# Another order of the same 578 pieces: layer norm, local dilated attention and a gelu MLP on one core

## The chip, the cores and the metric

The kernel runs on one core of one Trainium2 chip. The metric is the device time of one execution in microseconds, lower is better. The median of six runs of the kernel before is 212.39 us (212.2 to 212.59).

## What is computed

One layer-normed input feeds an attention branch and an MLP branch, and both are added to the input:

```python
xn = _layernorm(x)                       # x: 2048 x 640, bf16
# A: q, k, v = xn @ wqkv; 32 heads of 20; each position looks at itself and at
#    the 7 positions 2, 4, ... 14 before it (W = 8, dilation 2), softmax over these 8
logits = einsum("bhsd,bhswd->bhsw", q, kg) * scale
attn   = softmax(where(mask, logits, -1e9))
o      = einsum("bhsw,bhswd->bhsd", attn, vg);   A = o @ wo
# B: 640 -> 1536 -> 640
B      = gelu(xn @ w1 + b1) @ w2 + b2
return x + A + B
```

## The kernel before

The 2048 positions are cut into four chunks of 512, numbered 0 to 3 (n), and each chunk into four blocks of 128 (bl). Features lie on the partitions, positions along the free axis. Everything runs in small **pieces**, Python functions that each issue a few instructions. The list ORDER (from line 84) names every piece once, and the last lines of the kernel simply call the pieces in that order. Four engines (PE, DVE, ACT, SP) take their instructions in exactly the order of the list; each engine runs its own instructions strictly one after another, and semaphores make an instruction wait for what it needs from other engines. Only POOL is outside this: its instructions are placed by the framework. So ORDER fixes what each engine does next, and with it which instruction stands behind a waiting one.

Names of pieces that the text below uses (first digit: the chunk):

- `st`, `rs`, `rc`, `xn`: statistics (DVE), square root (ACT), reciprocal (DVE), normalised block (DVE for chunk 0, ACT for the others). `tp`, `tc` turn a block: on PE and by copies for chunk 0, by a DMA transpose on SP's queue for chunks 1 to 3 (line 477), into `xnT`.
- Projections: `pj{n}{q,k,v = 0,1,2}{to}` is five matmuls of 128x512 (line 509), and `pc...` is the ACT copy out of PSUM (line 568). In chunk 0 they are cut finer: `ga`, `gb*`, `gd`, `ge`, then `hj{q,k,v}{pair}{g}` of five or ten matmuls of 128x256 (line 553), with ACT copies `hc...` and `gc...`. `pad` fills the 14 columns that reach back into the chunk before.
- Attention on DVE: `qk{n}{w}{i}` multiplies q by the shifted k (line 583), eight per chunk; `lg{n}0` to `lg{n}3` sum over each head on PE (line 608); `m`, `mx`, `ex` (ACT), `ss`, `ri`, `at` are the softmax; `xd` (SP's queue) and `xs` (ACT's queue), two DMAs each at line 665, spread the weights `ax` over the 20 partitions of a head; `av` (eight, line 681), `ad` (three, line 690) and `ot` (line 696) form the attention output `oT`.
- MLP: `f1{n}{ft}` is five matmuls of 128x512 (line 703) and `ge{n}{ft}` the gelu on ACT (line 714).
- Output: `o{n}{bl}0` to `o{n}{bl}4` accumulate block bl in two PSUM banks `lo` and `hi` (lines 734 and 736); pieces 0 to 3 take three gelu tiles each, piece 4 takes `oT`, so piece 4 of the first block of a chunk waits for `ot`. `oc` (ACT, lines 741 and 742) copies out, `od` (POOL, line 747) adds the block to the output in DRAM. `xp` and `xb` put x and b2 into the output before that. The last block ends the kernel with `oclo`, `ohi` and `ochi`.

Buffers: four PSUM banks are shared by all `pj`, `f1` and `hj` outputs, so PE may run at most four such pieces ahead of ACT's copies. `lo`, `hi` and the logits have one place each. The products `prod` of `qk` and `av` share four buffers; `ax`, `oT` and the softmax tiles have one.

Weights come in at the start on SP's queue in the fixed order x block 0, wq, wk, x blocks 2 and 3, wv, the rest of x, w1 in two halves (from line 342). ACT needs a table load whenever it goes between square root, exp and gelu.

The lines that make the list into a program:

```python
        pieces = make_plan(fns).by
        assert sorted(ORDER) == sorted(pieces)
        for name in ORDER:
            pieces[name]["fn"]()
```

Of the kernel before, what the change touches and what calls it, by code (L numbers as in the profile page):

```python
# [82 lines left out]

ORDER = """
pad01 pad02 st00a st00 sm rs00 me nm rc00 sq xn00a xn00b tp00a tp00b tc00a rs01 tb ga tc00b rc01 xn01 gb2 b1 tp01
gb3 tc01a tc01b gb4 gd gc0 ge st03a hj101 gc4 st03 st02a rs03 hj102 st02 hc101 hj100 rs02 hc102 rc02 rc03 gc1 hj200
xn03 xn02 hc100 st11a tp03 tp02 st13a tc03 hj201 st11 tc02 st10a hj202 hc200 st12a hj012 st10 hj010 st13 hc012 hc202
st12 hj111 hc010 hc201 hj011 rs1 hc111 rc1 st21a hj110 hc011 st22a st22 hj112 hc110 st20a hj212 st33a hc112 f102
xn10 qk031 hc212 f100 xn13 tc10 qk001 ge02 f109 qk020 hj210 pad11 tc13 ge09 hj211 qk010 xn11 f108 hc211 qk000 ge00
f101 tc11 qk011 f105 ge01 ge08 qk021 f104 xn12 f1011 tc12 ge04 qk030 f1010 ge011 st23a st21 lg00 ge010 st20 ld lg01  # L90
ge05 st23 lg02 lg03 st31a rs2 pj114 mk m0 pj102 pc114 st32a st30a pj110 pc102 mx0 hc210 pj111 pc110 st32 ex0 pj101
rc2 st31 st30 pj100 st33 pj112 ss0 pc100 pc101 pj104 xn21 ri0 pj103 tc21 pc104 at0 pc111 pj113 pc103 pc112 pj123
pc113 xn23 qk120 f113 pc123 tc23 xn22 f103 qk111 pj121 ge03 qk121 f118 xd0 qk130 ge13 f107 ge18 f112 qk100 ge07
pad21 f106 ge12 qk110 xs0 f115 ge06 qk131 xw0 f110 rs3 qk101 o020 tc22 xn20 o021 ge15 lg10 lg11 av011 lg12 pc121
tc20 lg13 ge10 rc3 pj120 av000 o022 pc120 av031 xn32 o023 pj122 tc32 av021 f111 pc122 m1 xn30 pj124 ge11 av030 tc30
pad12 pj214 av020 pj204 pc214 pj203 pc204 av001 pj211 pc203 av010 pc124 pj202 xn33 mx1 pc211 pj210 tc33 xn31 ad01
pj221 pc210 pc202 pj223 tc31 pj201 ad00 pj220 pc201 pc223 pj213 xp0 pj200 pc213 ad02 pc221 pj212 pc220 pc200 pj224
pc212 ex1 xb0 ot0 pj310 f1110 qk231 pc310 o024 qk220 pj300 oc02 ss1 pad31 od02 o000 o001 qk200 o002 o003 ri1 o004
at1 pj313 qk201 xd1 oc00 o010 pc313 qk211 pc300 pj301 xs1 qk210 o011 o012 qk221 o013 xw1 pj303 qk230 o014 xp1 xb1
lg20 oc01 lg21 av130 pc303 lg22 pc224 lg23 av100 o030 f138 av110 o031 od00 ge38 av111 pj312 o032 pc301 m2 ge110 f117  # L100
pc312 av131 f116 av120 pj304 pj302 mx2 o033 pc302 av121 ge16 f121 ge17 ad11 f1111 xp2 f1210 ge21 xb2 ge111 o034
ge210 av101 pad22 pc304 f119 ad10 pj311 pj222 pc311 xb3 oc03 pj314 ad12 ge19 od01 f114 od03 f125 ge14 pc222 ot1
pj324 pad32 pc314 ex2 o100 qk331 pj322 qk321 o101 ge25 o102 ss2 o103 pj323 ri2 o104 qk330 pc323 pc322 pj320 at2 oc10
pj321 pc320 qk311 xd2 xs2 o110 pc324 qk301 o111 pc321 o112 qk310 f120 qk300 f126 xw2 f130 ge26 qk320 f127 xl lg30
ge27 lg31 av201 lg32 lg33 o113 m3 o114 av211 f1311 oc11 av200 od11 o120 o121 od10 av221 o122 av230 o123 o124 av220
f1211 oc12 mx3 od12 o130 av210 o131 ge20 ge30 f124 ex3 ad20 f123 o132 ge311 o133 av231 o134 ge24 ss3 f128 ge211 oc13
f129 ad21 ge23 f122 ge29 ge28 f131 ge22 ri3 o210 at3 f135 ad22 o211 xd3 f134 f1310 ot2 o212 ge310 ge31 o213 xs3 o214
xw3 f137 oc21 ge34 od21 o220 av311 o221 o222 av300 o223 av310 o224 f136 av321 oc22 od22 o230 av301 o231 od13 o232
av320 o233 av331 o234 av330 f132 oc23 od23 o200 ad31 o201 ge32 ge36 o202 ge37 f139 ad30 f133 ge39 ge35 o203 ge33
o204 ad32 o310 oc20 o311 o300 ot3 o301 o302 o303 o304 o312 oc30 o313 od30 o320 od20 o321 o322 o323 o314 o324 oc31  # L110
od31 o330 oc32 o331 od32 o332 o333 o334 ohi oclo ochi
""".split()


# [696 lines left out]
```

## Time and profile before

| | before |
| --- | --- |
| median of six runs (lowest, highest) | 212.39 us (212.2, 212.59) |
| the profiled execution | 212.2 us |
| its span, first to last instruction | 210.2 us |
| PE matmuls busy | 205.2 us, 98% of the span |
| DVE busy | 173.4 us, 82% |
| ACT busy | 111.6 us, 53% |
| POOL busy | 19.8 us, 9% |
| DMA traffic | 23.93 MB, mean 114 GB/s |

The span is what the trace covers; 2.0 us of the profiled execution's time lie around it. Busy times of engines overlap. A PE row's duration is that of one matmul from start to end, and matmuls are pipelined, so the distance from one start to the next, not the duration, is what a matmul costs in a row of them. In the rows of the timeline, the first column is the start in us, the second the time from the first start to the last end, and a bracket at the end says how long the engine stood idle before and what ended it.

### The profile page before, as it was taken

The page shows a single profiled execution, that of the slowest core. Times are in us where ns is not written, and L with a number is a line of the kernel's source. Part 1 is how long each engine was busy: PE and PEld are TensorE (multiplying, and loading weights), DVE is VectorE, ACT ScalarE, POOL GpSimd, SP SyncE. Part 2 cuts the span into 40 slices and gives each one's busy share as a digit, 9 for nine tenths or more (in the row PEclk, how much of TensorE's full clock was granted, in tenths as well). Part 3 has the DMA queues.
Part 4 walks back from the last instruction along what each step waited for, and adds up shares of the span by engine and source line. Part 5 has one row for each costly group of instructions (what it writes and reads, how often), then busy time and mean ns, then how long its engine had stood idle before and what let it go on. Part 6 is the DMA issues. An engine that isn't in the chain of part 4 may idle for free.

```text
span 210.2 us, 3645 instructions
## 1 busy us (share of the span) xinstructions
PE 205.2 (98%) x1511; PEld 118.5 (56%) x1535; DVE 173.4 (82%) x178; ACT 111.6 (53%) x193; POOL 19.8 (9%) x37
## 2 busy tenths in 40 slices
PE   8999999999999999999999999999999999999994
PEld 2999646554465555555654555565554455555552
DVE  3587999969979999996999999969999929997001
ACT  5477977899785849230717486321396221441120
POOL 2000000000000002110400600101101011101130
PEclk9999999999999999999999999999999999999999
DMA  6999427915862074569296790731212572212224
GB/s 216 366 362 372 91 36 203 379 44 92 139 65 54 9 189 46 84 95 232 64 153 219 97 152 3 122 110 11 27 27 34 100 125 18 28 27 31 31 25 72
DMA packets 24072, 23.93 MB, mean 114 GB/s; under 512 B 9080, under 2 KB 21880, under 8 KB 24056
## 3 DMA queue, kind: packets, MB, share of 16 engines
q1 hardware_dynamic: 17008, 14.68, 26.4%
q0 software_dynamic: 4144, 4.92, 17.7%
q10 hardware_dynamic: 2904, 4.10, 7.1%
q8 instruction: 12, 0.20, 0.4%
q14 instruction: 4, 0.03, 0.1%
HBM read 10.00 MB, written 7.54 MB: 83 GB/s over the span
## 4 chain that ended last, share of the span: by engine, by line
PE 96%; DMA 1%; issue 1%; ACT 1%; DVE 0%
PE lo L734 27%; PE hps L703 25%; PE pps L509 23%; PE hi L736 8%; PE gps L553 6%; PE L L608 4%; PE gps L522 1%; DMA x_sb<-in_A_x_dram 1%; PE tp L465 1%; ACT xn L417 0%; DVE xn L450 0%; ACT std L430 0%; DVE osb L764 0%; DVE rstd L434 0%; ACT L376 0%
## 5 line engine op out<-in xcount | busy, mean ns | idle before, releaser
L703 PE MATMUL hps<-xnT,w_sb 128*128 128x512 bf16 x235 | 55.1, 379 | 0.3
L681 DVE TENSOR_TENSOR pv<-vT,ax 128x2560 bf16<-128x2560 bf16 x32 | 45.9, 1485 | 9.2 <-DMA ax<-attn 8.0
L734 PE MATMUL lo<-w_sb,hT 128*128 128x512 bf16 x184 | 52.9, 379 | 0.1
L583 DVE TENSOR_TENSOR prod<-qT,kT 128x2560 bf16<-128x2560 bf16 x32 | 45.5, 1485 | 1.9 <-ACT kT L568 1.5
L714 ACT ACTIVATE hT<-hps,b1T 128x512 bf16<-128x512 f32 x48 | 31.6, 688 | 19.9 <-PE hps L703 18.5
L736 PE MATMUL hi<-w_sb,hT 128*128 128x128 bf16 x192 | 40.3, 219 | 0.5 <-issue 0.2
L703 PEld LDWEIGHTS <-w_sb 128*128 128x128 bf16 x240 | 22.8, 98 | 26.1 <-DMA w_sb<-in_B_w_dram 0.3
L690 DVE TENSOR_TENSOR pv<-pv 128x5120 bf16<-128x5120 bf16 x12 | 33.7, 2822 | 0.2
L741 ACT CAST osb<-lo 128x512 bf16<-128x512 f32 x15 | 8.8, 586 | 44.7 <-issue 26.7
L734 PEld LDWEIGHTS <-hT 128*128 128x128 bf16 x192 | 18.7, 98 | 22.5 <-issue 0.4
L734 PE MATMUL lo<-wo,oT 128*128 128x512 bf16 x74 | 21.9, 379 | 0.0
L747 POOL DMA_DIRECT2D out_dram<-osb x15 | 13.6, 904 | 86.4 <-ACT osb L742 80.2
L736 PEld LDWEIGHTS <-hT 128*128 128x128 bf16 x192 | 18.4, 98 | 2.7
L509 PE MATMUL pps<-xnT,wk_sb 128*128 128x512 bf16 x73 | 18.2, 379 | 0.1
L509 PE MATMUL pps<-xnT,wv_sb 128*128 128x512 bf16 x72 | 18.0, 379 | 0.1
L509 PE MATMUL pps<-xnT,wq_sb 128*128 128x512 bf16 x75 | 18.0, 379 | 0.1
L736 PE MATMUL hi<-wo,oT 128*128 128x128 bf16 x80 | 16.9, 219 | 0.3
L409 DVE BATCH_NORM_STATS2 stats<-x_sb 128x6 f32<-128x320 bf16 x30 | 13.0, 468 | 4.4 <-DMA x_sb<-in_A_x_dram 4.4
L490 POOL DMA_DIRECT2D out_dram<-b2bc x4 | 5.3, 1466 | 98.1 <-DMA out_dram<-x_sb 98.1
L568 ACT CAST qT<-pps 128x512 bf16<-128x512 f32 x15 | 8.7, 590 | 8.8 <-PE pps L509 8.8
L734 PEld LDWEIGHTS <-oT 128*128 128x128 bf16 x80 | 7.8, 98 | 9.4
L509 PEld LDWEIGHTS <-wk_sb 128*128 128x128 bf16 x75 | 8.6, 118 | 7.3 <-issue 0.2
(75 smaller groups left out, 198.5 us busy)
## 6 DMA issues: line engine op xcount, KB each, us to landing
w_sb<-in_B_w_dram SPq DMA_DIRECT2D x4, 960.0 KB, 11.1
out_dram<-osb POOLq DMA_DIRECT2D x15, 160.0 KB, 3.4
ax<-attn SPq DMA_DIRECT2D x8, 256.0 KB, 4.7
ax<-attn ACTq DMA_DIRECT2D x8, 256.0 KB, 4.3
out_dram<-b2bc POOLq DMA_DIRECT2D x3, 640.0 KB, 6.7
x_sb<-in_A_x_dram SPq DMA_DIRECT2D x1, 1280.0 KB, 13.6
out_dram<-x_sb ACTq DMA_DIRECT2D x1, 1120.0 KB, 4.6
wq_sb<-in_A_wqkv_dram SPq DMA_DIRECT2D x1, 800.0 KB, 4.8
```

The lines of the kernel that those rows point to most:

```text
L409: nc.vector.bn_stats(stats[:, i, :], x_sb[:, b, i * (D // 2) : (i + 1) * (D // 2)])
L509: nc.tensor.matmul(ps[:], lhsT=wqkv_p[which][:, ti, to, :], rhs=xnT[:, ti, :], start=(ti == 0), stop=(ti == KT - 1),)
L553: nc.tensor.matmul(ps[:, to - a, :], lhsT=wqkv_p[which][:, ti, to, :], rhs=tiles["xnT", 0][:, ti, pair * 2 * P : (pair + 1) * 2 * P], star ...
L583: nc.vector.tensor_tensor(out=prod[:, i, :, :], in0=qkv_tile(n, 0)[:], in1=qkv_tile(n, 1)[:, :, off : off + CH], op=ALU.mult,)
L681: nc.vector.tensor_tensor(out=pv[:, i, :, :].rearrange("p t (j c) -> p t j c", j=BPC), in0=qkv_tile(n, 2)[:, :, off : off + CH].rearrange( ...
L690: nc.vector.tensor_tensor(out=ta[:], in0=ta[:], in1=tb[:], op=ALU.add)
L703: nc.tensor.matmul(ps[:], lhsT=w1_sb[:, ti, ft * P : (ft + 1) * P], rhs=tiles["xnT", n][:, ti, :], start=(ti == 0), stop=(ti == KT - 1),)
L714: nc.scalar.activation(hT[:], tiles["hps", n, ft][:], ACT.Gelu_apprx_tanh, bias=b1T[:, ft : ft + 1], scale=1.0)
L734: nc.tensor.matmul(lo[:], lhsT=lhs, rhs=rhs[:, 0:CH], start=first, stop=last)
L736: nc.tensor.matmul(hi[:, 0 : D - CH], lhsT=lhs, rhs=rhs[:, CH:D], start=first, stop=last)
L741: nc.scalar.copy(osb[:, 0:CH], tiles["lo", n, bl][:])
L747: nc.gpsimd.dma_start(rows, tiles["osb", n, bl][:], accum_op=ALU.add)
```

## The change

Only the text of ORDER differs. The same names stand in it, each once, so every instruction is issued once as before, on the same engine, with the same operands. What changes is which comes after which on PE, DVE, ACT and SP, and through the rotating buffers which piece waits for which. The first 33 names are the same (up to `hj101`), and so are the last ten. Pieces that the text below speaks of, cut out of both lists (the numbers of the chunks are the first digits):

```diff
-gb3 tc01a tc01b gb4 gd gc0 ge st03a hj101 gc4 st03 st02a rs03 hj102 st02 hc101 hj100 rs02 hc102 rc02 rc03 gc1 hj200
+gb3 tc01a tc01b gb4 gd gc0 ge st03a hj101 gc1 st03 st02a rs03 hj100 st02 hc101 gc4 rc03 xn03 hj200 rs02 hc100 rc02
...
-pc113 xn23 qk120 f113 pc123 tc23 xn22 f103 qk111 pj121 ge03 qk121 f118 xd0 qk130 ge13 f107 ge18 f112 qk100 ge07
-pad21 f106 ge12 qk110 xs0 f115 ge06 qk131 xw0 f110 rs3 qk101 o020 tc22 xn20 o021 ge15 lg10 lg11 av011 lg12 pc121
+pc100 f112 pc113 xs0 qk121 f106 xd0 f118 qk120 ge06 f103 qk101 f107 ge03 qk130 pad21 f110 ge07 xw0 xn21 o020 qk100
+ge18 pj121 xn22 qk111 pj123 tc22 qk131 o021 pc123 ge12 f113 qk110 pc121 rs3 f115 tc21 lg10 ge10 rc3 lg11 av020 lg12
...
-at1 pj313 qk201 xd1 oc00 o010 pc313 qk211 pc300 pj301 xs1 qk210 o011 o012 qk221 o013 xw1 pj303 qk230 o014 xp1 xb1
+od00 pj310 qk210 xd1 o010 pc310 pj300 qk201 o011 qk230 pj313 o012 pc313 qk231 xs1 o013 o014 qk220 xw1 pj301 xp1 lg20
...
-pj324 pad32 pc314 ex2 o100 qk331 pj322 qk321 o101 ge25 o102 ss2 o103 pj323 ri2 o104 qk330 pc323 pc322 pj320 at2 oc10
-pj321 pc320 qk311 xd2 xs2 o110 pc324 qk301 o111 pc321 o112 qk310 f120 qk300 f126 xw2 f130 ge26 qk320 f127 xl lg30
+pc312 f126 ge210 ri2 f127 at2 ge26 o101 pc321 qk331 xd2 o102 pj324 ot1 f121 qk310 o103 o104 qk330 pj320 oc10 qk301
+ge27 od10 o110 qk321 pj222 o111 qk320 pc222 pc320 f130 xs2 qk311 f120 pc324 xw2 o112 qk300 f138 lg30 ge38 lg31 av231
...
-f129 ad21 ge23 f122 ge29 ge28 f131 ge22 ri3 o210 at3 f135 ad22 o211 xd3 f134 f1310 ot2 o212 ge310 ge31 o213 xs3 o214
-xw3 f137 oc21 ge34 od21 o220 av311 o221 o222 av300 o223 av310 o224 f136 av321 oc22 od22 o230 av301 o231 od13 o232
+at3 o134 ad20 xd3 f124 oc13 xs3 od13 f123 pad32 od11 f135 ge23 ad22 ge24 f134 ge29 o210 xw3 ge34 o211 ot2 o212 o213
+xl av321 o214 av320 f137 oc21 od21 o220 av301 o221 av331 o222 o223 av311 o224 av310 f136 oc22 od22 o230 av300 o231
```

Engine by engine this comes to the following. PE runs the q piece `hj102` and a v piece `hj212` later in chunk 0, so the first v piece `hj200` is two pieces (ten and ten matmuls) behind `ge` instead of three; from there the projections, `f1` and `o` pieces stand in other places, with the four `lg` groups after the same amount of PE work as before. DVE takes the softmax of chunk 1 (`m1`, `mx1`) after the attention output of chunk 0 instead of between its products, the sums, reciprocals and weights of chunk 2 (`ss2`, `ri2`, `at2`) before `ot1` instead of after it, and those of chunk 3 (`ss3`, `ri3`, `at3`) directly after the products of chunk 2, ahead of its `ad20` and `ad22`. SP issues `xd0` after one transpose of chunk 2 instead of two, and `xp0` between the transposes of chunk 3 instead of after them. ACT has `xs0`, `xs1`, `xs2`, `xs3` at new places, and `xs0` now stands directly before a gelu with a table load. ACT loads a table 12 times after the first in either order. POOL's sequence of output DMAs is the same.

More of the change, by code (lines that the diff above doesn't have):

```diff
@@ L85 @@
 pad01 pad02 st00a st00 sm rs00 me nm rc00 sq xn00a xn00b tp00a tp00b tc00a rs01 tb ga tc00b rc01 xn01 gb2 b1 tp01
-gb3 tc01a tc01b gb4 gd gc0 ge st03a hj101 gc4 st03 st02a rs03 hj102 st02 hc101 hj100 rs02 hc102 rc02 rc03 gc1 hj200
-xn03 xn02 hc100 st11a tp03 tp02 st13a tc03 hj201 st11 tc02 st10a hj202 hc200 st12a hj012 st10 hj010 st13 hc012 hc202
-st12 hj111 hc010 hc201 hj011 rs1 hc111 rc1 st21a hj110 hc011 st22a st22 hj112 hc110 st20a hj212 st33a hc112 f102
-xn10 qk031 hc212 f100 xn13 tc10 qk001 ge02 f109 qk020 hj210 pad11 tc13 ge09 hj211 qk010 xn11 f108 hc211 qk000 ge00
@@ L90 @@
-f101 tc11 qk011 f105 ge01 ge08 qk021 f104 xn12 f1011 tc12 ge04 qk030 f1010 ge011 st23a st21 lg00 ge010 st20 ld lg01
-ge05 st23 lg02 lg03 st31a rs2 pj114 mk m0 pj102 pc114 st32a st30a pj110 pc102 mx0 hc210 pj111 pc110 st32 ex0 pj101
-rc2 st31 st30 pj100 st33 pj112 ss0 pc100 pc101 pj104 xn21 ri0 pj103 tc21 pc104 at0 pc111 pj113 pc103 pc112 pj123
-pc113 xn23 qk120 f113 pc123 tc23 xn22 f103 qk111 pj121 ge03 qk121 f118 xd0 qk130 ge13 f107 ge18 f112 qk100 ge07
-pad21 f106 ge12 qk110 xs0 f115 ge06 qk131 xw0 f110 rs3 qk101 o020 tc22 xn20 o021 ge15 lg10 lg11 av011 lg12 pc121
@@ L95 @@
[L95 to L98, printed above, removed]
-at1 pj313 qk201 xd1 oc00 o010 pc313 qk211 pc300 pj301 xs1 qk210 o011 o012 qk221 o013 xw1 pj303 qk230 o014 xp1 xb1
@@ L100 @@
-lg20 oc01 lg21 av130 pc303 lg22 pc224 lg23 av100 o030 f138 av110 o031 od00 ge38 av111 pj312 o032 pc301 m2 ge110 f117
-pc312 av131 f116 av120 pj304 pj302 mx2 o033 pc302 av121 ge16 f121 ge17 ad11 f1111 xp2 f1210 ge21 xb2 ge111 o034
-ge210 av101 pad22 pc304 f119 ad10 pj311 pj222 pc311 xb3 oc03 pj314 ad12 ge19 od01 f114 od03 f125 ge14 pc222 ot1
-pj324 pad32 pc314 ex2 o100 qk331 pj322 qk321 o101 ge25 o102 ss2 o103 pj323 ri2 o104 qk330 pc323 pc322 pj320 at2 oc10
-pj321 pc320 qk311 xd2 xs2 o110 pc324 qk301 o111 pc321 o112 qk310 f120 qk300 f126 xw2 f130 ge26 qk320 f127 xl lg30
@@ L105 @@
-ge27 lg31 av201 lg32 lg33 o113 m3 o114 av211 f1311 oc11 av200 od11 o120 o121 od10 av221 o122 av230 o123 o124 av220
-f1211 oc12 mx3 od12 o130 av210 o131 ge20 ge30 f124 ex3 ad20 f123 o132 ge311 o133 av231 o134 ge24 ss3 f128 ge211 oc13
-f129 ad21 ge23 f122 ge29 ge28 f131 ge22 ri3 o210 at3 f135 ad22 o211 xd3 f134 f1310 ot2 o212 ge310 ge31 o213 xs3 o214
-xw3 f137 oc21 ge34 od21 o220 av311 o221 o222 av300 o223 av310 o224 f136 av321 oc22 od22 o230 av301 o231 od13 o232
-av320 o233 av331 o234 av330 f132 oc23 od23 o200 ad31 o201 ge32 ge36 o202 ge37 f139 ad30 f133 ge39 ge35 o203 ge33
@@ L110 @@
-o204 ad32 o310 oc20 o311 o300 ot3 o301 o302 o303 o304 o312 oc30 o313 od30 o320 od20 o321 o322 o323 o314 o324 oc31
-od31 o330 oc32 o331 od32 o332 o333 o334 ohi oclo ochi
+gb3 tc01a tc01b gb4 gd gc0 ge st03a hj101 gc1 st03 st02a rs03 hj100 st02 hc101 gc4 rc03 xn03 hj200 rs02 hc100 rc02
+xn02 tp03 tp02 st10a tc03 hj201 st12a tc02 st11a hj202 st13a hc200 st10 hj010 st12 hj011 st13 hc010 st11 hc201 hj110
+hc011 st22a st21a hc202 hj111 st22 hc110 st20a hj012 st20 hc111 hj112 rs1 hj102 rc1 hc112 hc012 hj211 hc102 xn10
@@ new lines @@
+qk011 f104 xn13 tc10 qk031 f101 ge04 f108 qk000 ge01 hj210 tc13 ge08 qk020 f1011 hc210 xn11 qk030 f109 ge011 tc11
+hj212 qk010 f1010 hc212 xn12 qk001 f105 ge09 tc12 f100 ge05 qk021 ge010 f102 ge00 st23a st21 lg00 ge02 ld st23 lg01
+st31a lg02 rs2 lg03 pj112 mk st30a hc211 st31 pj101 pad12 pc112 st32a m0 pj102 pc101 pad11 st30 pj103 pc102 mx0
+pj114 pc103 st33a ex0 pj110 st32 rc2 st33 pj111 pc114 pj104 ss0 xn23 pj100 pc110 tc23 ri0 pc111 pj113 pc104 at0
+pc100 f112 pc113 xs0 qk121 f106 xd0 f118 qk120 ge06 f103 qk101 f107 ge03 qk130 pad21 f110 ge07 xw0 xn21 o020 qk100
@@ new lines @@
+ge18 pj121 xn22 qk111 pj123 tc22 qk131 o021 pc123 ge12 f113 qk110 pc121 rs3 f115 tc21 lg10 ge10 rc3 lg11 av020 lg12
+lg13 av021 xn20 pj120 tc20 pj122 av011 o022 pc122 av000 ge15 o023 ge13 f1110 av030 xn33 f111 tc33 av010 pj124 ge11
+av001 pj212 pc124 pj213 av031 pc212 pj223 pc213 ad01 xn31 pj210 pc120 tc31 pj200 pc210 pad22 pj204 ad00 pc200 pj214
+pc204 xp0 pc223 pj220 pc214 ad02 pj203 pc220 xn32 pj202 pc203 xb0 tc32 pj211 pc202 ot0 pj224 pc211 xn30 m1 pj201
+pc224 tc30 mx1 o024 pc201 qk221 pj221 oc02 ex1 o000 qk200 o001 qk211 o002 pc221 o003 ss1 o004 ri1 pj303 oc00 at1
@@ new lines @@
+od00 pj310 qk210 xd1 o010 pc310 pj300 qk201 o011 qk230 pj313 o012 pc313 qk231 xs1 o013 o014 qk220 xw1 pj301 xp1 lg20
+pc301 xb1 lg21 av131 pc300 lg22 oc01 lg23 pad31 av121 f116 o030 av101 pj314 ge16 av120 od01 o031 ge110 o032 av111
+pc314 f117 m2 f1111 ge17 pc303 av110 f125 ge111 o033 ge25 av100 pj304 av130 f114 pc304 xp2 pj311 ad10 xb2 f119 pc311
+pj302 ad11 o034 pc302 pj323 oc03 ge19 pj312 mx2 xb3 ge14 pc323 f1210 ad12 ex2 od02 o100 od03 pj322 pj321 ss2 pc322
+pc312 f126 ge210 ri2 f127 at2 ge26 o101 pc321 qk331 xd2 o102 pj324 ot1 f121 qk310 o103 o104 qk330 pj320 oc10 qk301
@@ new lines @@
+ge27 od10 o110 qk321 pj222 o111 qk320 pc222 pc320 f130 xs2 qk311 f120 pc324 xw2 o112 qk300 f138 lg30 ge38 lg31 av231
+lg32 lg33 av220 o113 o114 m3 f1311 oc11 av210 ge21 o120 mx3 o121 o122 av221 ex3 o123 av230 o124 f1211 ad21 oc12 od12
+o130 o131 ge211 o132 av200 o133 ge20 av211 f128 ge30 f122 ge28 av201 f1310 ss3 f131 ge310 ge311 ri3 f129 ge31 ge22
+at3 o134 ad20 xd3 f124 oc13 xs3 od13 f123 pad32 od11 f135 ge23 ad22 ge24 f134 ge29 o210 xw3 ge34 o211 ot2 o212 o213
+xl av321 o214 av320 f137 oc21 od21 o220 av301 o221 av331 o222 o223 av311 o224 av310 f136 oc22 od22 o230 av300 o231
@@ L112 @@
+av330 o232 o233 ad31 o234 f132 oc23 od23 ad30 o200 o201 ge37 ge32 f133 ge36 ge35 o202 ad32 ge33 o203 f139 o204 ge39
+o310 ot3 oc20 o311 od20 o300 o301 o302 o303 o304 o312 oc30 o313 od30 o320 o321 o314 o322 oc31 o323 od31 o324 o330
+oc32 o331 od32 o332 o333 o334 ohi oclo ochi
 """.split()
```

## The prediction

> **What bounds the kernel now.** I read the page's busy times and slices first, then the list of waits for PE alone, then the timelines of PE, DVE, ACT and SP at the places that the change touches.
>
> ```profile
> PE 205.2 (98%) x1511; PEld 118.5 (56%) x1535; DVE 173.4 (82%) x178; ACT 111.6 (53%) x193; POOL 19.8 (9%) x37
> PE   8999999999999999999999999999999999999994
> PEclk9999999999999999999999999999999999999999
> PE 96%; DMA 1%; issue 1%; ACT 1%; DVE 0%
> ```
>
> ```profile
> PE idle L776 <- PEq L795: 0.8, 1, 0.8
> PE hi L736 <- issue: 0.2, 1, 0.2
> ```
>
> The first fence says that PE is busy in every slice at full clock and that the chain that ends last is PE's. The second is PE's whole list of waits: 0.8 us at the start of the program and 0.2 us later. Between the first transposes at 5.3 us and the last matmul that starts at 207.5 us, PE waits for nobody worth a name. The distances in the rows agree: five 128x512 matmuls take 1.08 us (216 ns from start to start), a `lo`/`hi` pair 0.27 us. Since both orders hold the same matmuls, this sum stays, and a new order can win only what PE waits today: at most the 0.2 us. It can lose wherever something now comes late for PE. So the question is where the new order puts a piece ahead of its input.
>
> Here the Trainium skill disagrees: "TensorE: Matmul & The Clock Gate", section "Back-to-back issue gap", gives about 131 ns for a sustained 128x512 matmul, and counts 216 ns as the isolated gap. By that figure my estimate is that the 737 such matmuls (225 in `pj`, 240 in `f1`, 272 into `lo`) could cost about 63 us less, and PE would not be at its floor; no row here shows less than 216 ns, and the order does not touch the spacing in either case.
>
> **How I place the new order.** I lay PE's pieces end to end: 1.08 us for `pj` and `f1`, 0.81 us for `o` pieces 0 to 3 and 1.36 us for piece 4, 0.109 us for a 128x256 matmul. The `lg` groups have the same PE work ahead of them in both orders, so their rows (58.9, 99.45, 139.46 us) serve as fixed points, from which I count backwards or forwards. The other engines follow from their own rows.
>
> ```profile
> 9.17 2.89 PE L553 MATMUL gps<-xnT,wk_sb 128*128 128x256 bf16 x25
> 11.89 1.25 PE L553 MATMUL gps<-xnT,wv_sb 128*128 128x256 bf16 x10
> ```
>
> ```profile
> 2.80 0.53 SPq L345 DMA_DIRECT2D wv_sb<-in_A_wqkv_dram  x1
> ```
>
> ```profile
> wv_sb<-in_A_wqkv_dram SPq DMA_DIRECT2D x1, 800.0 KB, 8.8
> ```
>
> **1. The first v piece, a new wait.** wv is issued at 2.80 us and lands 8.8 us later, at 11.6. Today 25 wk matmuls run from 9.17 and the first wv matmul at 11.89 finds it landed, 0.3 us early. The new order has only 20 ahead of it (`hj102` is moved back): 9.17 + 20 x 0.109 = 11.35. PE waits 11.6 - 11.35 = **0.25 us**. Bounds: nothing if wv lands a quarter earlier in an ordinary run; at most 11.89 - 11.35 = 0.54, since PE found it there at 11.89. I take 0.25. All of PE's queue stands behind this wait, and nothing later has a fixed time that could take it back: w1, the next load, is first needed some 0.5 us later than today. So it goes to the end.
>
> ```profile
> 140.92 1.49 DVE L681 TENSOR_TENSOR pv<-vT,ax 128x2560 bf16<-128x2560 bf16 x1 [1.76 <-DMA ax<-attn]
> ...
> 166.43 1.49 DVE L696 TENSOR_TENSOR oT<-pv 128x2560 bf16<-128x2560 bf16 x1
> 171.93 11.30 DVE L681 TENSOR_TENSOR pv<-vT,ax 128x2560 bf16<-128x2560 bf16 x8 [4.01 <-DMA ax<-attn]
> 183.27 8.42 DVE L690 TENSOR_TENSOR pv<-pv 128x5120 bf16<-128x5120 bf16 x3
> 191.80 1.49 DVE L696 TENSOR_TENSOR oT<-pv 128x2560 bf16<-128x2560 bf16 x1
> ```
>
> ```profile
> 166.81 0.69 ACT L714 ACTIVATE hT<-hps,b1T 128x512 bf16<-128x512 f32 x1 [5.18 <-PE hps L703]
> 167.02 0.57 ACTq L665 DMA_DIRECT2D ax<-attn  x1
> 167.39 0.68 ACT L714 ACTIVATE hT<-hps,b1T 128x512 bf16<-128x512 f32 x1
> 167.63 0.61 ACTq L665 DMA_DIRECT2D ax<-attn  x1
> ```
>
> **2. The attention output, moved slack.** Brackets name `ax` as DVE's release. From ACT's first issue to DVE's start: 4.9 us in chunk 3 (167.02 to 171.93) and at most 5.5 in chunk 0 (54.12 to 59.65), where SP's pair went 3 to 5 us earlier; at most 7.5 in chunk 1 (92.86 to 100.35) and 9.1 in chunk 2 (131.81 to 140.92), where both pairs went together or 1.7 us apart. I use 4.9 where the new order holds the pairs apart and 9.1 where it does not.
>
> - Chunk 1, `ot1` for `o104`. `xs1` now stands behind `pc313`; `pj313` is 5.14 us of pieces before `lg20`, so it ends at 95.4 and ACT issues at 95.7, SP's pair 4 us ahead. `ax` at 100.6. Then DVE has eight `av` (11.3), three `ad` (8.4), `m2` and `mx2` (2.3), `ss2`, `ri2`, `at2` (3.6), one `qk` (1.4) and `ot1` (1.5): 28.5, ready at 129.1. `o104` is 9.19 us of pieces before `lg30`, at 130.3. Margin 1.2 us; today `ot1` ends at 124.1 against `o104` at 129.2, margin 5. This is what the softmax sums ahead of `ot1` cost.
> - Chunk 2, `ot2` for `o214`. DVE does the same set from its first `av` to the end of `ot2` as in the rows 140.92 to 167.92: 27.0 us. `xs2` goes behind the copies of `pj222`, which ends at 134.6: issue 134.9, `ax` at 139.8; `lg30` frees the product buffer at about 140.2. Ready at 167.2 against `o214` at 168.4. Margin 1.2, today 0.5.
> - Chunk 3, `ot3` for `o304`. `at3` is earlier, and `xs3` goes at about 161.2, but together with SP's pair: 161.2 + 9.1 = 170.3. From there 21.4 us as in the rows 171.93 to 193.29: 191.7 against `o304` at 193.7. Margin 2.0, today 0.45.
> - Chunk 0: `xs0` at 46.7 + 9.1 = 55.8, while DVE is on its products until 58.4.
>
> So all four fit; cost **0**, bounds 0 and 2.9 us (chunk 1 at 9.1 us).
>
> **3. ACT behind its own DMA issues.** A pair of issues holds ACT's queue for 1.2 us (chunk 3) to 2.1 us (chunk 1). `xs0` at 46.7 is now followed by a table load and `ge06`, which has to free a bank for `f107`. By the lengths of the rows below: 46.7 + 1.2 + 1.29 + 0.69 = 49.9 against `f107` at 50.75; with 2.1, 50.8. `xs3` delays `ge23`, which frees a bank for `f134` at 164.06: with 1.2 done at 163.8, with 2.1 at 164.2. Cost **0**, bounds 0 and 0.2 us.
>
> ```profile
> 49.22 1.28 ACT L714 ACT_TABLE_LOAD   x1
> 50.51 2.07 ACT L714 ACTIVATE hT<-hps,b1T 128x512 bf16<-128x512 f32 x3
> ```
>
> The gelu starts 1.29 us after the load starts. The Trainium skill, "ScalarE: Activation LUTs", section "What ACT_TABLE_LOAD costs", puts a switch at about 2.66 us with its drain; by that estimate `ge06` would be 1.4 us later and `f107` would stall 0.5 to 1.4 us. The rows decide against it.
>
> **4. The rest.** The projections, `f1` and `o` pieces change places, with the same four banks; the ACT copy that frees a bank is, as today, one to three pieces ahead of its need, and today's such places (`o010` behind `oc00`, `f121` behind `pc302`) show no gap. Chunk 3's transposes now stand on either side of `xp0`; the last, issued near 82, has to land by `pj303` at about 89, against 2.6 to 5.0 us to landing. Chunk 2's wait behind `xd0`; the last, near 62, is due at 68. POOL's sequence is the same, the table loads are 12 either way, and the last ten pieces are the same, so the 2.7 us after the last matmul stay. Cost 0, bounds -0.2 (the waits above) and +0.2.
>
> **Sum.** 212.2 for the profiled execution, of which 210.2 are span, + 0.25 = 212.45. The median stands 0.2 above it: 212.6 to 212.7. I say **212.6 us**. Differences under 0.2% (0.42 us) are about what a measurement of this kernel can tell from no change; that band is 211.97 to 212.81.
>
> **Rivals.**
> - *Slower: `ax` of chunk 1 is late.* If it takes as long as in chunk 1 today (7.5), DVE starts at 103.2, `ot1` is ready at 131.7, and `o104`, itself 0.25 late, waits 1.1: 213.7 us. At 9.1 us it is 215.3. It decides from 6.4 us after the issue. For it: `xp1` is again issued directly behind. Against: SP's pair is out of the way. Chance 0.15.
> - *Slower: ACT's queue is held longer,* at `xs0` and `xs3`, or copies come late in step 4: 0.2 to 0.8 on top of 0.25, 212.8 to 213.4. Chance 0.16.
> - *It does nothing:* wv lands by 11.35, or the larger margin at `o304` pays in runs where `ax` of chunk 3 is later than in this trace, which is worth at most the 0.2 between median and fastest run: 212.2 to 212.4. Chance 0.14.
> - *Faster,* under 211.97: PE would have to drop 0.42 us, and its whole list of later waits is 0.2. Chance 0.05.
> - Forecast, 212.45 to 212.8: 0.50.
>
> **How the numbers follow.** Same: 0.50 + 0.14 = 0.64. Slower: 0.15 + 0.16 = 0.31. Faster: 0.05. The range 212.1 to 213.7 leaves out the faster case and the upper half of the late `ax`, some 0.13, and takes in the bounds of steps 1, 3 and 4.
>
> **What would show it.** In the new profile PE should have one new wait, 0.25 us, for wv near 11.4; no wait for `ot` or a bank; the last matmul near 207.7; `ot1` ending near 129, `ot3` near 191 or before. Step 2 is wrong if PE waits at its first `lo<-wo,oT` near 130 or 168; step 3 if it waits near 50.8 or 164. The whole is wrong if the last matmul starts before 207.2 or after 208.2.

## The result and the profile after

The kernel after takes 213.67 us in the median (213.33 to 215.53, 34 runs), the kernel before 212.44 us (212.17 to 214.89, 70 runs). The ratio is 1.0057, 95% interval 1.0045 to 1.0069: slower by 1.2 us. The profiled execution took 213.44 us with a span of 211.5 us, against 212.2 and 210.2 us.

The page of after: busy times, and the chain that ended last by engine.

```profile
PE 205.6 (97%) x1511; PEld 118.3 (56%) x1535; DVE 173.6 (82%) x178; ACT 111.8 (53%) x193; POOL 19.8 (9%) x37
PE 91%; ACT 2%; ACTq 2%; issue 2%; DMA 1%; DVE 1%
```

And PE's waits in after (us in total, times, longest).

```profile
PE idle L776 <- PEq L795: 0.8, 1, 0.8
PE hps L703 <- ACT hT L714: 0.7, 2, 0.4
PE tp L465 <- DVE xn L450: 0.2, 1, 0.2
PE hi L736 <- issue: 0.2, 1, 0.2
```

PE's busy time is as before. New are two waits of a hidden-layer matmul for a gelu, 0.7 us together, and in the chain 2% of the span (some 4 us) of ACTq, that is ACT issuing DMAs. Before, the chain was PE's for 96% and ACT had 1%.

The place is found with the fixed points that the prediction uses, the rows of the sums `lg` (line 608), in front of which both orders have the same PE work.

| from ... to | before | after | difference |
| --- | --- | --- | --- |
| start of the span to `lg` of chunk 0 | 33.18 | 33.35 | +0.17 |
| `lg` of chunk 0 to `lg` of chunk 1 | 25.63 | 26.25 | **+0.62** |
| `lg` of chunk 1 to `lg` of chunk 3 | 80.58 | 80.56 | -0.02 |
| `lg` of chunk 3 to the end of the last matmul | 68.09 | 68.53 | **+0.44** |
| sum | 207.48 | 208.69 | +1.21 |

Two stages hold nearly all of it, and each holds one of the two new waits. The chain of waits of after, between 46 and 54 us (start, us, what), shows the first from cause to effect.

```profile
46.68 0.58 ACT kT L568
47.26 0.30 ACTq L665
...
47.60 1.73 ACTq L665
...
49.36 1.28 ACT L714
...
50.66 0.69 ACT hT L714
...
51.39 2.32 PE hps L703 x10
```

Read from the bottom: PE's matmuls at 51.39 (`f107`) wait for the gelu at 50.66 (`ge06`) to free a bank. That gelu waits for its table load at 49.36, and the load stands behind the second ax DMA of `xs0`, whose issue alone takes 1.73 us. The first began at 46.91, so the pair lasts 2.42 us. The same place in ACT's timeline of after:

```profile
46.68 0.58 ACT L568 CAST kT<-pps 128x512 bf16<-128x512 f32 x1 [0.33 <-PE pps L509]
46.91 2.42 ACTq L665 DMA_DIRECT2D ax<-attn  x2
49.36 1.28 ACT L714 ACT_TABLE_LOAD   x1 [2.10 <-issue]
```

PE's timeline has a break there in after (the first two rows; one matmul's record is missing from the first), and an unbroken row of thirty matmuls in before (the third):

```profile
46.48 4.48 PE L703 MATMUL hps<-xnT,w_sb 128*128 128x512 bf16 x19
51.39 2.32 PE L703 MATMUL hps<-xnT,w_sb 128*128 128x512 bf16 x10 [0.44 <-ACT hT L714]
50.62 6.64 PE L703 MATMUL hps<-xnT,w_sb 128*128 128x512 bf16 x30
```

The matmul before the wait starts at 50.58 and the next at 51.39: 0.82 us instead of 0.216, so 0.60 us lost, nearly the whole of the stage's 0.62. (The bracket of 0.44 counts only from the end of the matmul before, 0.379 us after its start.)

The second place is `xs3`. ACT's timeline of after:

```profile
161.88 0.57 ACTq L665 DMA_DIRECT2D ax<-attn  x1
162.11 0.27 ACT L742 CAST osb<-hi 128x128 bf16<-128x128 f32 x1
162.49 1.69 ACTq L665 DMA_DIRECT2D ax<-attn  x1
164.22 0.25 ACT L575 COPY vT<-vT 128x70 bf16<-128x70 bf16 x1 [1.84 <-issue]
164.38 1.84 ACT L714 ACTIVATE hT<-hps,b1T 128x512 bf16<-128x512 f32 x3
```

And PE's for the same place:

```profile
165.11 1.24 PE L703 MATMUL hps<-xnT,w_sb 128*128 128x512 bf16 x5 [0.27 <-ACT hT L714]
```

Again the second issue is long (1.69 us). The bracket of 1.84 us "issue" is ACT's engine with nothing to do while its queue issues. The gelus behind it come late, and `f134` starts at 165.11 instead of 164.68, where it would start without a gap: 0.43 us, the second stage's loss.

### The profile page after: what moved, and what is told of

Read it like the earlier page. It is cut to its first block, busy times and chain, and to the rows that moved or that the text cites. A ratio compares the mean times of both kernels' runs of the same rounds, so it can differ in the third digit from the quotient of the medians.

```text
span 211.5 us, 3636 instructions
## 1 busy us (share of the span) xinstructions
PE 205.6 (97%) x1511; PEld 118.3 (56%) x1535; DVE 173.6 (82%) x178; ACT 111.8 (53%) x193; POOL 19.8 (9%) x37
## 4 chain that ended last, share of the span: by engine, by line
PE 91%; ACT 2%; ACTq 2%; issue 2%; DMA 1%; DVE 1%
PE lo L734 26%; PE pps L509 23%; PE hps L703 21%; PE hi L736 8%; PE gps L553 6%; PE L L608 4%; ACTq L665 2%; PE gps L522 1%; DMA x_sb<-in_A_x_dram 1%; ACT hT L714 1%; PE tp L465 1%; ACT L714 1%; DVE stats L409 0%; ACT kT L568 0%; DVE xn L450 0%
## 5 line engine op out<-in xcount | busy, mean ns | idle before, releaser
L714 ACT ACTIVATE hT<-hps,b1T 128x512 bf16<-128x512 f32 x48 | 30.9, 687 | 14.4 <-PE hps L703 13.1
L734 PE MATMUL lo<-wo,oT 128*128 128x512 bf16 x77 | 22.5, 379 | 0.1
L747 POOL DMA_DIRECT2D out_dram<-osb x15 | 14.4, 957 | 86.6 <-ACT osb L742 79.9
L509 PE MATMUL pps<-xnT,wq_sb 128*128 128x512 bf16 x72 | 17.5, 379 | 0.1
L755 DVE TENSOR_TENSOR osb<-lo,x_sb 128x512 bf16<-128x512 f32 x1 | 0.7, 692 | 16.1 <-PE lo L734 16.1
L568 ACT CAST kT<-pps 128x512 bf16<-128x512 f32 x15 | 8.7, 587 | 9.1 <-PE pps L509 9.1
```

Source lines behind the costliest of these rows:

```text
L509: nc.tensor.matmul(ps[:], lhsT=wqkv_p[which][:, ti, to, :], rhs=xnT[:, ti, :], start=(ti == 0), stop=(ti == KT - 1),)
L568: nc.scalar.copy(dest[:, to, off : off + CH], tiles["pps", n, which, to][:])
L714: nc.scalar.activation(hT[:], tiles["hps", n, ft][:], ACT.Gelu_apprx_tanh, bias=b1T[:, ft : ft + 1], scale=1.0)
L734: nc.tensor.matmul(lo[:], lhsT=lhs, rhs=rhs[:, 0:CH], start=first, stop=last)
L747: nc.gpsimd.dma_start(rows, tiles["osb", n, bl][:], accum_op=ALU.add)
```

## The experiments

**The theories.** A: the two DMA issues of `xs0` and `xs3` hold ACT's queue, the gelus behind them free banks late, and PE waits. B: the new order of the table load, the banks and the `f1` pieces makes the waits, and the DMA issues only stand beside them. C: the loss is made of many small ones. In the runs below the first inputs often landed later than in the profiles of before and after, and before itself varies more (its median is 213.17 us beside the first four, then 212.53, then 212.70). So each run is read by its time, as a ratio to the runs of before taken beside it, and, where the time can't tell, by the stage distances of its profile. These ratios with their intervals are not quotients of the medians shown.

**1. `xs0` alone later.** The order after, with `xs0` behind `ge03`:

```diff
-pc100 f112 pc113 xs0 qk121 f106 xd0 f118 qk120 ge06 f103 qk101 f107 ge03 qk130 pad21 f110 ge07 xw0 xn21 o020 qk100
+pc100 f112 pc113 qk121 f106 xd0 f118 qk120 ge06 f103 qk101 f107 ge03 xs0 qk130 pad21 f110 ge07 xw0 xn21 o020 qk100
```

> The changed kernel with one name moved: xs0 (ACT's two ax issues of chunk 0) from behind pc113 to behind ge03. The table load stays directly in front of ge06. Theory A (ACT's queue is held 2.4 us by the two issues, so ge06 frees a bank late and f107 waits 0.6 us): the table load starts near 47.2 instead of 49.4, PE has no wait near 51, and the kernel is about 0.6 us faster than the changed one, 213.0 to 213.1. Theory B (the order of the projections and gelus around the table load leaves too few free banks, and the issues only happen to stand there): f107 still waits, 213.6. Theory C (the time is lost elsewhere in many small places): no change beyond 0.2 us.

**2. `xs3` alone later**, behind `ge29`:

```diff
-at3 o134 ad20 xd3 f124 oc13 xs3 od13 f123 pad32 od11 f135 ge23 ad22 ge24 f134 ge29 o210 xw3 ge34 o211 ot2 o212 o213
+at3 o134 ad20 xd3 f124 oc13 od13 f123 pad32 od11 f135 ge23 ad22 ge24 f134 ge29 xs3 o210 xw3 ge34 o211 ot2 o212 o213
```

> The changed kernel with xs3 moved from behind oc13 to behind ge29. Theory A: the second wait, 0.4 us at f134 near 165, goes, and nothing else changes: about 0.45 us faster, 213.2. The price is a later ax in chunk 3: DVE starts av3 near 170.5 instead of 170.2, which is covered. Theory B: ge23 is late by its own place behind oc13, the wait stays, 213.6.

**3. Both moves together.**

> The changed kernel with both xs0 and xs3 moved as in the two kernels above. Theory A: both waits gone, about 1.05 us faster than the changed kernel, 212.6, within 0.2 us of the kernel before. Theory C: clearly above the kernel before by more than 0.5 us still, with the lost time spread over the span.

**4. All ax DMAs on SP's queue**, the order after untouched (`xs` is left empty):

```diff
-        expand(nc.sync, n, (0, 1))
+        expand(nc.sync, n, range(BPC))
...
-        expand(nc.scalar, n, (2, 3))
+        pass
```

> The changed kernel's order untouched, but all four ax issues of each chunk come from SP's queue and ACT issues none (xs is empty). Theory A: ACT is never held, so both waits of PE vanish although no piece has moved: 212.6, like the kernel before. Theory B: the waits at f107 and f134 stay, 213.6. A third outcome, the last ax landing 1 to 2 us later because four issues stand in one queue, would show as a wait of PE at o104 or o214.

Measured, one line for each profile (the row of before has the 70 runs of the result; the stage distances are differences of the starts of the `lg` rows; the last is to the end of the last matmul):

| kernel | median us (lowest) | ratio to before, 95% | `lg` 0 to 1 | `lg` 3 to end | PE's waits for a gelu |
| --- | --- | --- | --- | --- | --- |
| before | 212.44 (212.17) | | 25.63 | 68.09 | none |
| after | 213.67 (213.33) | 1.0057 [1.0045, 1.0069] | 26.25 | 68.53 | 0.7 in 2 |
| 1: `xs0` later | 213.72 (212.99) | 1.0039 [1.0000, 1.0078] | 25.65 | 68.53 | 0.3, near 165 |
| 2: `xs3` later | 213.93 (213.03) | 1.0054 [1.0022, 1.0086] | 26.28 | 68.10 | 0.5, near 52 |
| 3: both later | 213.59 (212.69) | 1.0038 [1.0004, 1.0073] | 25.66 | 68.09 | none |
| 4: all on SP | 213.18 (212.44) | 1.0000 [0.9959, 1.0041] | 25.65 | 68.10 | none |

Each move takes away exactly its own stage's loss and leaves the other, and both together bring both stages back to before within 0.03 us. In 1 to 4 the table load and the `f1` pieces still stand in the order after, and in 4 ORDER is not touched at all: B has fallen. `lg` 1 to 3 is 80.55 to 80.58 us in all six rows, so C has nothing there.

The times alone decide less. The expected 213.0, 213.2 and 212.6 us of runs 1 to 3 did not come (213.72, 213.93, 213.59), beside a before of 213.17; as ratios, the intervals of all three hold what A expects and also the 1.0057 of after. Only 4 is told apart from after by its time, and narrowly (its interval ends at 1.0041, that of after begins at 1.0045). Run 3 still lies 0.4% above before, with both stages restored. In its profile the extra time stands ahead of the first `lg`: that row starts at 36.29 us, against 33.18 in before and 33.35 in after (34.15, 34.11 and 34.10 in runs 1, 2 and 4), with a wait of 1.4 us for wq and a granted clock of about 0.75 between 5 and 12 us. Whether the new order makes this first part slower on average isn't shown.

In run 4 PE's longest wait but the idle start is 0.6 us for the load of wq, and no gelu is in its list; such waits for the first loads differ from run to run.

**5. SP's pair later.** Why does `xs0` take 2.42 us, where pairs of before took 1.2 to 2.1? In after, SP issues its own pair, `xd0`, at the same time (46.90 us). So, in the order after, `xd0` goes behind `tc22` (the 41.5 us in the expectation is not the distance it names, which is 26.25 us in after):

```diff
-pc100 f112 pc113 xs0 qk121 f106 xd0 f118 qk120 ge06 f103 qk101 f107 ge03 qk130 pad21 f110 ge07 xw0 xn21 o020 qk100
-ge18 pj121 xn22 qk111 pj123 tc22 qk131 o021 pc123 ge12 f113 qk110 pc121 rs3 f115 tc21 lg10 ge10 rc3 lg11 av020 lg12
+pc100 f112 pc113 xs0 qk121 f106 f118 qk120 ge06 f103 qk101 f107 ge03 qk130 pad21 f110 ge07 xw0 xn21 o020 qk100
+ge18 pj121 xn22 qk111 pj123 tc22 xd0 qk131 o021 pc123 ge12 f113 qk110 pc121 rs3 f115 tc21 lg10 ge10 rc3 lg11 av020 lg12
```

> The order after with one piece moved: xd0 (SP's pair of weight DMAs of chunk 0) goes from in front of f118 to behind the transpose tc22, so that SP issues its pair some us later than ACT issues xs0. Theory A says that ACT's hold at xs0 is the cause of PE's wait near 51. A1, the second issue on ACT is long (1.73 us of 2.42 us) because SP issues its own pair at the same moment: the hold falls to about 1.2 us, gelus of ge06 and ge03 come 1.2 us earlier, the wait of 0.44 us at the L703 row near 51 goes to 0, the step from lg of chunk 0 to lg of chunk 1 goes from 41.5 less what the wait took to that of before, and the time falls by 0.4 to 0.6 us against the order after. A2, the length belongs to the DMA or to ACT alone and not to SP's issue: the pair stays at 2.3 to 2.5 us, the wait stays at 0.4 to 0.6 us, the time stays that of the order after within 0.1 us. Either way the wait before f134 near 165 stays at 0.2 to 0.45 us.

213.92 us at the lowest, 214.27 in the median, ratio 1.0077 [1.0040, 1.0115]. ACT's timeline in this run:

```profile
49.60 1.29 ACTq L665 DMA_DIRECT2D ax<-attn  x2
50.92 1.28 ACT L714 ACT_TABLE_LOAD   x1 [0.97 <-issue]
```

The pair takes 1.29 us, no matmul near 51 waits, and `lg` 0 to 1 is 25.66: for the hold, A1 came true. The time went the other way, because SP's pair was now too late (58.97 us): PE's waits have 1.1 us for `oT` of chunk 0 (at 86.35), and `lg` 1 to 3 is 81.89 instead of 80.56. The expected gain of 0.6 was there and was paid back twice over in the next stage.

**6. The head.** Run 4 with `hj102` and its copy moved back ahead of `hj100`:

```diff
-gb3 tc01a tc01b gb4 gd gc0 ge st03a hj101 gc1 st03 st02a rs03 hj100 st02 hc101 gc4 rc03 xn03 hj200 rs02 hc100 rc02
+gb3 tc01a tc01b gb4 gd gc0 ge st03a hj101 gc1 st03 st02a rs03 hj102 hj100 st02 hc101 gc4 rc03 xn03 hj200 rs02 hc102 hc100 rc02
...
-hc011 st22a st21a hc202 hj111 st22 hc110 st20a hj012 st20 hc111 hj112 rs1 hj102 rc1 hc112 hc012 hj211 hc102 xn10
+hc011 st22a st21a hc202 hj111 st22 hc110 st20a hj012 st20 hc111 hj112 rs1 rc1 hc112 hc012 hj211 xn10
```

> The order after with all four weight DMAs of a chunk on SP's queue, and with the q piece hj102 and its copy hc102 where they stand in the order before, so that the first v piece again has three pieces of q behind ge. If the head's part of the loss is the narrower margin to wv, PE waits 0 for wv in the L553 rows and the distance from the first wk matmul to the first lg of chunk 0 is 24.0 us as in before (24.09 in the profile of after, 24.2 in the profile with all on SP); from lg of chunk 0 to the end 174.1 us as in before. Time then equal to before within 0.1 us. If the margin has nothing to do with it, the distance stays at 24.1 to 24.2 us. A time under that of before by over 0.2 us would say that PE's matmuls are not the floor.

212.96 us (lowest 212.35), ratio 1.0027 [0.9994, 1.0059]. PE does not wait for wv, but that tells little: in this profile wq came 1.4 us late, so that wv was there in any case, as in run 3. From the first wk matmul to the first `lg` it is 24.2 us, not 24.0: a gap of 0.19 us appears at 28.2 us instead, where a v piece starts 0.05 us after the end of the first gelu that follows a table load. The expectation for the distance failed. Run 6 does not say what the margin to wv is worth.

**7. `xs0` early in the order before.** If issuing a pair always holds ACT, the loss can be made in before:

```diff
-pc113 xn23 qk120 f113 pc123 tc23 xn22 f103 qk111 pj121 ge03 qk121 f118 xd0 qk130 ge13 f107 ge18 f112 qk100 ge07
-pad21 f106 ge12 qk110 xs0 f115 ge06 qk131 xw0 f110 rs3 qk101 o020 tc22 xn20 o021 ge15 lg10 lg11 av011 lg12 pc121
+pc113 xn23 qk120 f113 pc123 tc23 xn22 xs0 f103 qk111 pj121 ge03 qk121 f118 xd0 qk130 ge13 f107 ge18 f112 qk100 ge07
+pad21 f106 ge12 qk110 f115 ge06 qk131 xw0 f110 rs3 qk101 o020 tc22 xn20 o021 ge15 lg10 lg11 av011 lg12 pc121
```

> The order before with one piece moved: xs0 from behind ge12 to directly behind xn22, in front of the table load that starts at 49.22 us, where SP's pair is issued at 49.23 us too. Nothing else is touched. Theory A, ACT's queue is held: the first gelu ends the hold later than 51.2 us, and the fifth matmul piece from there, which starts at 51.70 us in before, finds its bank taken. With a hold of 2.4 us PE waits some 1.9 us at an L703 row and the kernel is 1.6 to 2.0 us slower; with a hold of 1.2 us it waits 0.7 us and is 0.6 to 0.8 us slower. Theory B, the order of banks, table loads or other moved pieces of the order after make the wait near 51: here PE waits 0 and the time is that of before within 0.1 us.

212.59 us against 212.53, ratio 0.998 [0.9939, 1.0022]; `lg` 0 to 1 is 25.64. Theory A expected 0.6 to 2.0 us more and got nothing, so A as it stood was wrong. SP's pair came late here (50.71 us instead of 49.23), and ACT's pair took 1.30 us, not 2.42; so it is the lower figure, 0.6 to 0.8 us, that failed. ACT's timeline in this run shows why:

```profile
47.19 0.92 ACT L446 ACTIVATE xn<-x_sb,nmr,rstd 128x640 bf16<-128x640 bf16 x1
47.88 0.65 ACTq L665 DMA_DIRECT2D ax<-attn  x1
48.01 0.57 ACT L568 CAST vT<-pps 128x512 bf16<-128x512 f32 x1
48.48 0.93 ACT L446 ACTIVATE xn<-x_sb,nmr,rstd 128x640 bf16<-128x640 bf16 x1
48.57 0.61 ACTq L665 DMA_DIRECT2D ax<-attn  x1
49.42 1.28 ACT L714 ACT_TABLE_LOAD   x1
```

`xs0` stands behind all three of these compute instructions in the list, yet its first issue starts at 47.88, before the copy at 48.01 and the norm at 48.48. So ACT's instructions don't run strictly one after another in the order of the list when DMA issues are among them. The queue hands instructions to the engine and goes on; the issues ran beside work that the engine already had, and the table load follows the norm without a bracket. In after there was no such work: the copy ahead of `xs0` had itself just waited for PE.

**8. Two norms ahead of `xs0`, in the order after.** This tells a queue that is simply busy from one that runs ahead:

```diff
-pc100 f112 pc113 xs0 qk121 f106 xd0 f118 qk120 ge06 f103 qk101 f107 ge03 qk130 pad21 f110 ge07 xw0 xn21 o020 qk100
-ge18 pj121 xn22 qk111 pj123 tc22 qk131 o021 pc123 ge12 f113 qk110 pc121 rs3 f115 tc21 lg10 ge10 rc3 lg11 av020 lg12
+pc100 f112 pc113 xn21 xn22 xs0 qk121 f106 xd0 f118 qk120 ge06 f103 qk101 f107 ge03 qk130 pad21 f110 ge07 xw0 o020 qk100
+ge18 pj121 qk111 pj123 tc22 qk131 o021 pc123 ge12 f113 qk110 pc121 rs3 f115 tc21 lg10 ge10 rc3 lg11 av020 lg12
```

> The order after with two ACT pieces that wait for nothing, xn21 and xn22 (0.91 us each), moved from behind ge07 and ge18 to directly in front of xs0. It tells apart two readings of ACT's queue. Reading 1, the issues of a DMA pair are time of ACT like any other instruction: then 1.7 to 1.8 us of work more stand in front of the table load, it starts near 51.1 us instead of 49.36, the first gelus come as much later, PE's wait at the L703 row near 51 grows from 0.4-0.6 to 2.2-2.4 us, and the kernel is 1.5 to 1.8 us slower than the order after. Reading 2, ACT's queue goes ahead of its engine: the issues start as soon as the waits of the instructions in front of them are over and run beside work that is already handed to the engine; only the part of the issues that lasts longer than that work holds the engine (by this the hold is 2.10 us at xs0 of after and 1.84 at its xs3, 0.97 in the run with SP's pair late, 0.76 with xs0 behind ge03, 0 with xs3 behind ge29 and 0 with xs0 behind xn22 in the order before). Then the issues start near 46.9 us as before, beside the two norms, the table load starts at 49.3 to 49.5 us as in after, the idle time of ACT in front of it falls from 2.1 to 0.2-0.4 us, PE's wait stays at 0.4 to 0.6 us, and the time is that of the order after within 0.1 us.

214.01 us (lowest 213.57), ratio 1.0073 [1.0030, 1.0115], which holds the ratio of after. ACT's timeline in this run:

```profile
47.62 0.64 ACTq L665 DMA_DIRECT2D ax<-attn  x1
47.65 0.92 ACT L446 ACTIVATE xn<-x_sb,nmr,rstd 128x640 bf16<-128x640 bf16 x1
48.30 1.60 ACTq L665 DMA_DIRECT2D ax<-attn  x1
48.47 0.91 ACT L446 ACTIVATE xn<-x_sb,nmr,rstd 128x640 bf16<-128x640 bf16 x1
49.93 1.28 ACT L714 ACT_TABLE_LOAD   x1 [0.55 <-issue]
```

1.8 us of work more stands in front of the table load, and the bracket in front of it shrinks from 2.10 to 0.55 us (0.2 to 0.4 expected). PE's wait at `f107` is 0.52 us (after: 0.44), `lg` 0 to 1 is 26.34 (26.25). So 1.8 us of work cost 0.09 us: reading 2 holds, reading 1 does not.

## Why the prediction was right or wrong

The time lies in the range (213.67 in 212.1 to 213.7), but by luck: the range reaches so far up for a late `ax` of chunk 1, which did not come. The forecast of 212.6 us failed, since the kernel is 1.2 us slower where up to 0.42 us was to count as no change, and so did its own test: the last matmul starts at 208.5, outside 207.2 to 208.2. (The 207.5 us that the prediction reads as the start of the last matmul in before is its end, 207.48; it starts at 207.26. Either way it comes 1.2 us later now.) What came true is the rival "ACT's queue is held longer", which had a chance of 0.16, with its place and its mechanism, and somewhat beyond its price (a median of 213.67 us against 212.8 to 213.4).

- **The floor.** Right. PE's matmuls cost the same in both orders, nothing was won, and none of the eight kernels of the experiments was faster than before by more than its interval.
- **Step 1, wv.** The direction was right and the size too large: 0.25 us expected. In the profile of after wv lands at 11.45 us, and the matmuls there lose 0.08 us in all (0.155 and 0.140 us from start to start at 11.34 and 11.50 instead of 0.109). In other profiles with this head the same place lost 0.2 us (run 4) to 0.4 us (run 2), so the bounds of 0 to 0.54 held. The other 0.1 us of the head lies ahead of the first wk matmul (9.27 against 9.17 us), where both orders are the same; in run 7, which has the head of before, it starts at 9.37, so this looks like a difference between executions.
- **Step 2, the attention output.** Right: no wait for `ot`. In chunk 1 `ax` released DVE 5.5 us after ACT's issue (4.9 taken). In after, DVE's rows are

```profile
101.83 2.90 DVE L681 TENSOR_TENSOR pv<-vT,ax 128x2560 bf16<-128x2560 bf16 x2 [2.80 <-DMA ax<-attn]
128.56 1.49 DVE L696 TENSOR_TENSOR oT<-pv 128x2560 bf16<-128x2560 bf16 x1
```

  so `ot1` ends at 130.05, 0.8 us ahead of PE's `o104` at 130.85 (1.2 expected). The margins of chunks 2 and 3 were 1.2 and 3.2 us (1.2 and 2.0 expected). (The prediction's margin of 0.5 us for chunk 2 in before is 0.3: `ot2` ends at 167.92, `o214` starts at 168.24.) The rival that needed `ax` of chunk 1 over 6.4 us did not come.
- **Step 3, ACT behind its own DMA issues: the step that failed.** The place, the chain and even the two times that it named as the sign of being wrong (near 50.8 or 164) were right: PE waits at 50.8 and 164.7. The term was mis-sized: 0 with bounds 0 and 0.2 us was set down, 1.06 us is what it cost (0.62 + 0.44). Two things made it so. The hold was taken as 1.2 us, the row of chunk 3, and at most 2.1; both pairs lasted longer (2.42 and 2.30 us), and both start within 0.8 us of SP's pair. With the pairs moved apart they lasted 1.29 us (`xs0` in run 5) and 1.22 us (`xs3` in run 2). The prediction had used just that for the landing of `ax` ("together with SP's pair") and not for ACT's own time. And its sums left little: by the hold of 2.1 us, `ge06` is done at 50.8 where `f107` needs it at 50.75, and `ge23` at 164.2 where `f134` needs it at 164.06. With no margin left, what came on top was a wait in full: at `xs0`, 0.3 us more of hold and 0.2 us more of start.
- **The table load.** The rule weighed there gives way to the rows again: the load at 49.36 takes 1.28 us, and the gelu starts 1.30 us after it ("ScalarE: Activation LUTs", section "What ACT_TABLE_LOAD costs", in the Trainium skill has about 2.66 with drain).
- **Step 4.** Right: `lg` 1 to 3 differs by 0.02 us.

## What to carry to other kernels

In these runs a DMA issue on ACT's queue cost ACT only the part that outlasted the work already handed to it. So look for a place behind instructions that wait for nothing, and avoid one directly behind an instruction that has just waited and in front of one that frees a buffer for the engine at its floor: two such places cost 1.06 us here. When two queues are made to issue the same set of DMAs at one moment, price the later issues by a row where that happened, and add that price to the issuing engine as well as to the landing.

## What the runs showed of the hardware

**A queue that runs ahead.** What ACT's engine stands idle after a pair is the end of the pair's issue less the end of the work handed over before it. In the six places looked at: 49.33 - 47.26 = 2.1 us in after at `xs0` (bracket 2.10); 164.18 - 162.38 = 1.8 at `xs3` (1.84); 50.89 - 49.95 = 0.9 in run 5 (0.97); 53.14 - 52.48 = 0.7 in run 1 (0.76); 49.90 - 49.38 = 0.5 in run 8 (0.55); and none in run 7, where the issue ends before the work does.

**The third and fourth DMA of a set.** An ax DMA is issued in 0.54 to 0.66 us when it is the first or second of its chunk's four, in every run but for one case (below). Run 4, with all four on SP, shows that the length is not a matter of two engines at once. SP's timeline, chunk 2:

```profile
126.72 0.54 SPq L665 DMA_DIRECT2D ax<-attn  x1
127.32 0.60 SPq L665 DMA_DIRECT2D ax<-attn  x1
127.97 1.19 SPq L665 DMA_DIRECT2D ax<-attn  x1
129.20 1.66 SPq L665 DMA_DIRECT2D ax<-attn  x1
```

All four chunks of run 4 have this shape (third 1.2 to 1.3, fourth 1.4 to 1.7). With two queues at once only one of the four is long (1.73 and 1.69 us in after; in chunk 0 of run 7 it was SP's, 1.98 us, in a pair 2.8 us behind ACT's), and with the pairs 3 us or more apart most often none (run 5: 0.64 and 0.61). What holds the later ones is open. It isn't settled by a count either: in run 7 the second DMA of a pair that stood alone took 1.30 us (chunk 3), and in before the four of chunk 2, all within 0.7 us, took no more than 0.83.
